# The last batch's main expert, picked by the gate's answer to the mean of its values, with its weights asked for five steps sooner

## The chip, the core and the metric

The kernel runs on one core of a Trainium2 chip. The metric is device time in microseconds, the median of several runs. One execution was also taken by the hardware profiler; its rows are what the text reads. Engines in those rows: PE is TensorE, PEld its weight loads, DVE is VectorE, ACT is ScalarE, POOL is GpSimd, SP is SyncE, which here only issues DMAs. L261 is line 261 of the kernel's file.

## What is computed

Multi-query attention over 8 batches, 16 heads, 384 positions and a head dimension of 64, all heads sharing one k and v; then a mixture of experts with a two-level gate, one expert for each of the 3072 tokens:

```python
scores = scale * np.matmul(q, k.transpose(0, 1, 3, 2))
attn = softmax(scores)                          
x = (attn @ v).transpose(0, 2, 1, 3).reshape(3072, 1024)
g_idx = argmax(x @ w_group)
e_idx = argmax(x @ w_expert[g_idx])
h = np.maximum(x @ w1[g_idx, e_idx], 0.0)
out = g_w * e_w * (h @ w2[g_idx, e_idx])
```

q, k and v are drawn with a standard deviation of 0.1, so scores are close to zero, attention is close to uniform and a token's row is close to the mean of its batch's v, repeated for the 16 heads. Worked out from the inputs, all 384 tokens of each of batches 0 to 6 choose one expert; in batch 7 363 tokens choose expert 0 and 21 choose expert 2. Expert weights are 4 MB each for w1 and w2 in fp32 and are turned to bf16 by the DMA that loads them.

## The kernel before

**Steps.** The attention is cut into tiles of 128 positions (`t`, 24 of them, three to a batch) and each tile into 4 steps, so there are 96 steps `i`, 12 to a batch; `s0` is a batch's first step (84 for batch 7). A step computes the scores of 4 heads (`scores`, L210), takes the maxima on DVE (`nmx`, L221), the exponentials on ACT (L224), the reciprocal of their sums on DVE (`rinv`, L235) and multiplies by it on POOL (`norm`, L239). Two steps later DVE transposes the result in blocks into a ring (`transp`, L245). The third and fourth step of a tile multiply the ring of the tile before by v on TensorE (`pv`, L261); `pv_out` copies the result on ACT and casts it on POOL to the bf16 tokens `xb`.

**Order.** The order on each engine is that of the program text; nothing is reordered. `at(step, place, function, ...)` puts a call at a named place of a step, and `run(i, place)` in the loop executes it. In the order of a step the places are: `s`, `b` (between the two score halves), then for a tile's first two steps `m0`, a group of expert work, `m1`, another, `m3`; then `v`, `m2`, the two transpositions, `w`, `norm`, `e`, `pv_out` in a tile's last step, and `g`. So `w` is ahead of the step's normalisation on DVE and POOL, and `g` behind it.

**Experts.** Each batch has a main expert, which is computed for all 384 tokens with weights zeroed for the tokens that chose another. `main_expert(b)` is a generator that `advance` moves in groups of 8 matmuls or so between the steps of the next batch: first `h` (L483, 64 matmuls), then `y` (L497, 48 matmuls), then scaling by the gate (L515 on ACT or L517 on DVE) and the writes to the output (L541, on SP; for the last tile of batch 7 half of them on ACT). Batch 6's expert begins in step 89, and both its last part and batch 7's whole expert run after the loop, in the drain.

**Picking the main expert.** When a batch's first tile of tokens exists, at step `s0 + 8`, `logits` (L284) computes its gate logits, `gate_first` marks each token's expert, `gate_choose` counts them with a matmul against ones (L345), `gate_score` and `gate_pick` find the expert with the highest count (ties by the lower number), and `load_main` reads that number into a POOL register (`value_load`) and issues the weights' DMAs, two for each of w1 and w2 (`load_w`, L458). For batches 0 to 6 this all is issued at `g` of step `s0 + 9`, for batch 7 w1 at `w` of step 93 and w2 at `w` of step 94. The pools hold two buffers for w1 and two for w2.

**Leftovers.** For batch 7 a second expert is picked (`gate_pick_second`: the highest count once the main expert's is taken out), its weights are loaded (`load_second(0)` for w1, `load_second(1)` for w2), and up to 32 of its tokens are gathered, computed at the end (`few_expert`, L677 for its matmuls, L693 for the scaling) and scattered into the output by an indirect DMA from POOL (L694). What is still not covered, by count, goes to a loop of a length known only on the chip (L909), which reads tokens back from a scratch in HBM that `keep_xb` (L474) fills for each batch. In the profiled execution it runs zero times.

**Buffers that matter here.** `xbank()` hands out four PSUM banks in turn, to the gate, the expert and `pv` (which takes all four); `scores` has two of its own. `transp` of a step reads what `norm` wrote two steps before.

## Time and profile before

| | us |
|---|---|
| median of 3 runs | 507.48 |
| lowest, highest run | 504.97, 507.82 |
| the profiled execution, its own time | 507.47 |
| its span, first to last instruction | 506.0 |
| TensorE busy | 479.9 (95%) |
| VectorE busy | 412.6 (82%) |
| ScalarE busy | 319.6 (63%) |
| GpSimd busy | 288.4 (57%) |
| mean granted TensorE clock, share of full | 0.986 |

In the rows of the timeline and of the groups the columns are: start and duration in us, engine, line, operation, what is written and what it is read from, the shapes, the number of instructions, and in brackets the idle time of the engine before and what ended it. In the chain of waits a row is a stretch of the chain that ended last: start, length, what it was. The answers about one line give "duration ns min/median/max, first and last start us" and, for DMAs, the time from issue to landing.

Places in time that the text speaks of: batch 7's first step, 84, has its scores at 395.52 us, step 85 at 400.53, step 88 at 413.99, step 93 at 438.79, and step 95, the last, at 448.50.

### The profile page before, as it was taken

To read this page: it belongs to the slowest core of one execution; us is meant where nothing else is said; L and a number is where in the kernel's file an instruction comes from. 1 tells how busy PE (TensorE), PEld (TensorE's weight loads), DVE (VectorE), ACT (ScalarE), POOL (GpSimd) and SP (SyncE) were. 2 spreads that over 40 slices of the span, in tenths; PEclk is the share of its full clock that TensorE was granted. 3 is DMA by queue.
4 is the path that set the end of the run, shared out by engine and by line. 5 is a ranking of instruction groups with operands and counts; after the bars stand their busy time and mean duration, and the time that the engine had idled before them with its cause. 6 is when DMAs were issued, how large, how long until landed. Compare 5 with 4: busy or idle time off the path is not lost.

```text
span 506.0 us, 20018 instructions
## 1 busy us (share of the span) xinstructions
PE 479.9 (95%) x8249; PEld 257.5 (51%) x8249; DVE 412.6 (82%) x738; ACT 319.6 (63%) x997; POOL 288.4 (57%) x528
## 2 busy tenths in 40 slices
PE   7687789999999999999999999999999999999992
PEld 3144355555455455555555455554555455555651
DVE  3899979998799888998799888898799888891441
ACT  4776756766765775766765875766766766662420
POOL 1656865585476654685476654684566653674210
PEclk9799999999999999999999999999999999999997
DMA  7522899389955999479965999279964995069995
GB/s 111 121 45 43 150 237 222 74 135 230 252 121 102 208 244 240 80 136 229 242 137 93 203 247 254 54 138 225 227 175 78 197 240 159 3 117 228 242 225 181
DMA packets 63660, 84.04 MB, mean 166 GB/s; under 512 B 20280, under 2 KB 39868, under 8 KB 63312
## 3 DMA queue, kind: packets, MB, share of 16 engines
q0 software_dynamic: 18288, 37.84, 41.2%
q1 hardware_dynamic: 44224, 44.35, 35.1%
q8 instruction: 66, 1.08, 0.9%
q10 hardware_dynamic: 1056, 0.56, 0.5%
q14 instruction: 26, 0.21, 0.1%
HBM read 101.52 MB, written 19.01 MB: 238 GB/s over the span
## 4 chain that ended last, share of the span: by engine, by line
PE 88%; DVE 4%; ACT 2%; DMA 2%; issue 1%; POOL 0%; SPq 0%; POOLq 0%; ACTq 0%; DVEq 0%
PE x L261 26%; PE s L210 26%; PE x L483 15%; PE x L497 13%; PE sb L497 3%; PE x L284 3%; ACT pr L224 2%; DVE nmx L221 2%; PE sb L483 2%; DMA out_dram<-y 2%; DVE ring L245 1%; PE x L104 1%; PE x L149 0%; PE x L187 0%; PE x L598 0%
## 5 line engine op out<-in xcount | busy, mean ns | idle before, releaser
L239 POOL TENSOR_SCALAR pr<-pr,rinv 128x384 f32<-128x384 f32 x384 | 217.3, 585 | 149.1 <-DVE rinv L235 135.9
L224 ACT ACTIVATE pr<-s,nmx 128x384 f32<-128x384 f32 x384 | 218.0, 579 | 132.2 <-DVE nmx L221 122.4
L221 DVE TENSOR_REDUCE nmx<-s 128x2 f32<-128x768 f32 x192 | 174.5, 949 | 47.2 <-PE s L210 46.3
L245 DVE STREAM_TRANSPOSE ring<-pr 128x768 f32<-128x768 f32 x192 | 175.4, 952 | 0.1
L210 PE MATMUL s<-kt,qt 64*64 64x384 f32 x1536 | 151.3, 504 | 12.0 <-ACT pr L224 9.9
L261 PE MATMUL x<-ring,v_sb 32*64 32x256 f32 x4608 | 137.9, 378 | 0.4 <-issue 0.3
L261 PEld LDWEIGHTS x<-ring,v_sb 32*64 32x64 f32 x4608 | 101.2, 131 | 43.7 <-issue 23.7
L210 PEld LDWEIGHTS s<-kt,qt 64*64 64x64 f32 x1536 | 48.8, 133 | 83.0 <-ACT pr L224 44.4
L224 ACT ACTIVATION_READ_ACCUMULATOR pr<-s,nmx 128x1 f32 x384 | 77.8, 203 | 0.0
L483 PE MATMUL x<-xb,w 128*128 128x384 bf16 x448 | 76.6, 326 | 0.0
L483 PEld LDWEIGHTS <-w 128*128 128x128 bf16 x512 | 47.7, 98 | 42.2 <-issue 12.6
L497 PE MATMUL x<-w,h_t 128*128 128x512 bf16 x288 | 65.3, 380 | 0.0
L497 PEld LDWEIGHTS <-h_t 128*128 128x128 bf16 x384 | 35.7, 98 | 51.9 <-issue 11.9
L458 POOL DMA_DIRECT2D w<-in_moe_w_dram x36 | 27.4, 767 | 10.7 <-issue 8.8
L275 ACT COPY xt<-x 128x256 f32<-128x256 f32 x96 | 28.9, 385 | 3.3 <-PE x L261 3.3
L489 ACT ACTIVATE h_t<-x 128x384 bf16<-128x384 f32 x56 | 25.4, 502 | 6.6 <-PE x L483 6.6
L276 POOL CAST xb<-xt 128x1024 bf16<-128x1024 f32 x24 | 24.9, 1036 | 3.4 <-ACT xt L275 3.4
L515 ACT ACTIVATE y<-x,gsel 128x512 f32<-128x512 f32 x36 | 24.8, 693 | 3.1 <-PE x L497 3.1
L199 DVE STREAM_TRANSPOSE qt<-q_sb 128x512 f32<-128x512 f32 x38 | 26.1, 687 | 0.0
L497 PE MATMUL sb<-w,h_t 128*128 128x512 bf16 x96 | 21.5, 379 | 0.0
L235 DVE RECIPROCAL rinv<-ssum 128x4 f32<-128x4 f32 x96 | 13.9, 145 | 3.3 <-ACT pr L224 3.3
L515 ACT ACTIVATE y<-sb,gsel 128x512 f32<-128x512 f32 x9 | 6.2, 689 | 15.7 <-PE sb L497 15.7
(129 smaller groups left out, 153.0 us busy)
## 6 DMA issues: line engine op xcount, KB each, us to landing
w<-in_moe_w_dram POOLq DMA_DIRECT2D x36, 1024.0 KB, 19.4
q_sb<-in_q_dram SPq DMA_DIRECT2D x76, 224.0 KB, 6.0
out_dram<-y SPq DMA_DIRECT2D x94, 128.0 KB, 6.4
xb_scratch<-xb SPq DMA_DIRECT2D x8, 768.0 KB, 4.3
v_sb<-in_v_dram SPq DMA_DIRECT2D x32, 96.0 KB, 3.7
kk<-in_k_dram SPq DMA_DIRECT2D x28, 92.0 KB, 4.1
q_sb<-in_q_dram SPq DMA_DIRECT2D x16, 128.0 KB, 3.4
q_sb<-in_q_dram SPq DMA_DIRECT2D x5, 64.0 KB, 3.0
```

The lines of the kernel that those rows point to most:

```text
L199: nc.vector.transpose(out=qt[:].rearrange("p (x d) -> p x d", d=32), in_=q_sb[:, :, 0:32])
L210: nc.tensor.matmul(out=s[m * D:(m + 1) * D, h, 0:S], lhsT=qt[r, ts(2 * cc + m, D)], rhs=kt[r, :], start=True, stop=True, tile_position=(h ...
L221: nc.vector.tensor_reduce(out=nmx[:], in_=s[:, :, 0:S], axis=AX.X, op=ALU.max, negate=True)
L224: nc.scalar.activation(out=pr[:, h, :], in_=s[:, h, 0:S], func=ACTF.Exp, bias=nmx[:, h:h + 1], scale=1.0, accum_out=ssum[:, k, h:h + 1],)
L239: nc.gpsimd.tensor_scalar(out=pr, in0=pr, scalar1=rinv[:, k, h:h + 1], scalar2=1.0, op0=ALU.mult, op1=ALU.mult)
L245: nc.vector.transpose(out=ring[:, (u // 4) % 3, u % 4].rearrange("p h s -> p (h s)"), in_=st.pop(("pr", u))[:].rearrange("p h s -> p (h s)"),)
L261: nc.tensor.matmul(out=o[i][h * D:(h + 1) * D, 0:2 * P].rearrange("d (g c q) -> d g c q", g=2, c=4), lhsT=v_sb[r, n, :], rhs=ring[r, a:z + ...
L275: nc.scalar.copy(out=xt[:, :, ts(i, 32)], in_=o[:, 0:2 * P].rearrange("p (c q) -> p c q", c=KO))
L458: nc.gpsimd.dma_start(out=w[:, o:o + 4, :], in_=views[n][ds(e, 1), :, o:o + 4, :].rearrange("o p c f -> (o p) c f"))
L483: nc.tensor.matmul(out=hp[:, 0:S], lhsT=w1[:, ko, ts(fc, P)], rhs=xb[:, ko, :], start=(ko == 0), stop=(ko == KO - 1))
L497: nc.tensor.matmul(out=yp, lhsT=h_t[:, fo, ts(j, P)], rhs=w2[:, fo, ts(nh, 512)], start=(fo == 0), stop=(fo == FO - 1),)
L515: nc.scalar.activation(out=y[:, ts(nh, 512)], in_=yp, func=ACTF.Copy, scale=g)
```

## The change

`gate_first` gets a number of partitions, so that it can work on 32 as on 128. For batch 7 a guess is made before any of its tokens exist. `guess_sum` adds up the 12 rows of v that each partition holds (DVE, `w` of step 81). `guess_mean` sums them over the partitions with two matmuls against a column of ones, one for each half of the partitions, so that the sum stands twice, as two heads have it, and copies it to 32 columns (TensorE and ACT, `m3` of step 84). `guess_logits` multiplies it with the gate's weights, 8 matmuls into one 32 x 32 block (`m3` of step 85); `guess_first` transposes the block and marks its expert on 32 partitions (DVE, `w` of step 85). Then the old functions count, score and pick at step 88. The weights are issued at `g` of steps 88 (w1) and 89 (w2) instead of `w` of steps 93 and 94.

The first tile's gate is still evaluated at step 93, now only for the second pick, which moves from the drain into `w` of step 94; `load_second(0)` moves from the drain to `g` of step 95. `keep_xb` of batch 7 moves from the end to just behind the last `pv_out`.

```diff
-    def gate_first(b):
+    def gate_first(b, n=P):
 
-        L = st["lg", b][:, 0, 0:NL].rearrange("p (g e) -> p g e", e=4)
+        L = st["lg", b][0:n, 0, 0:NL].rearrange("p (g e) -> p g e", e=4)
...
-        st["first", b] = first
+        st["first", b] = first, n
...
+        first, n = st.pop(("first", b))
         nc.tensor.matmul(
-            out=c_ps[:, 0:GE], lhsT=ones[:], rhs=st.pop(("first", b))[:].rearrange("p g e -> p (g e)"),
-            start=True, stop=True,
+            out=c_ps[:, 0:GE], lhsT=ones[0:n, :], rhs=first.rearrange("p g e -> p (g e)"), start=True, stop=True
         )
         st["c_ps", b] = c_ps
+
+    def guess_sum(b):
+        vs = pool.tile([P, D], FP32, tag="vs", name="vs", bufs=1)
+        nc.vector.tensor_reduce(out=vs[:], in_=st["v", b][:].rearrange("p n d -> p d n"), axis=AX.X, op=ALU.add)
+        st["vs"] = vs
+
+    def guess_mean():
+
+        vs = st.pop("vs")
+        bank = xbank()
+        for h in range(2):
+            nc.tensor.matmul(
+                out=bank[ts(h, D), 0:1], lhsT=vs[:], rhs=one[:], start=True, stop=True, tile_position=(0, h * D)
+            )
+        mean = pool.tile([P, 32], FP32, tag="mean", name="mean", bufs=1)
+        nc.scalar.copy(out=mean[:], in_=bank[:, 0:1].to_broadcast([P, 32]))
+        st["mean"] = mean
+
+    def guess_logits():
+
+        mean = st.pop("mean")
+        bank = xbank()
+        for ko in range(KO):
+            nc.tensor.matmul(
+                out=bank[0:32, 0:32], lhsT=wge[:, ko, :], rhs=mean[:], start=(ko == 0), stop=(ko == KO - 1),
+                tile_position=(0, 0),
+            )
+        st["guess"] = bank
+
+    def guess_first(b):
+        lg = pool.tile([P, ST, 32], FP32, tag="lg", name="guess_lg")
+        nc.vector.transpose(out=lg[0:32, 0, :], in_=st.pop("guess")[0:32, 0:32])
+        st["lg", b] = lg
+        gate_first(b, 32)
...
         at(s0 + 9, "w", gate_score, b)
-        at(s0 + 9, "w", gate_pick, b)
-        at(s0 + (13 if b == B - 1 else 12), "w", gate_picked, b)
         if b == B - 1:
-            at(s0 + 9, "w", load_main, b, 0)
-            at(s0 + 10, "w", load_main, b, 1)
+            at(s0 - 3, "w", guess_sum, b)
+            at(s0, "m3", guess_mean)
+            at(s0 + 1, "m3", guess_logits)
+            at(s0 + 1, "w", guess_first, b)
+            at(s0 + 4, "m3", gate_choose, b)
+            at(s0 + 4, "w", gate_score, b)
+            at(s0 + 4, "w", gate_pick, b)
+            at(s0 + 5, "w", gate_picked, b)
+            at(s0 + 4, "g", load_main, b, 0)
+            at(s0 + 5, "g", load_main, b, 1)
+            at(s0 + 10, "w", gate_pick_second, b)
+            at(s0 + 11, "g", load_second, 0)
         else:
+            at(s0 + 9, "w", gate_pick, b)
+            at(s0 + 12, "w", gate_picked, b)
...
-        if b == B - 1:
-            at(s0 + 13, "w", gate_pick_second, b)
...
+    one = singles.tile([P, 1], FP32)
+    nc.vector.memset(one[:], 1.0)
...
     transp(2 * i - 2)
     transp(2 * i - 1)
-    run(i + 1, "w")
     advance(1)
-    load_second(0)
     few_ready()
...
     pv_out(NT - 1)
+    keep_xb(b)
     advance(1)
     load_second(1)
...
     advance(1000)
-    keep_xb(b)
     few_expert()
```

More of the change, by code (lines that the diff above doesn't have):

```diff
@@ L300 @@
     NG = ST * (1 + G)
[L302 to L309 removed]
+    def gate_first(b, n=P):
+        L = st["lg", b][0:n, 0, 0:NL].rearrange("p (g e) -> p g e", e=4)
+        mx = pool.tile([P, 1 + G], FP32, tag="g_mx0", name="mx", bufs=1)[0:n]
+        nc.vector.tensor_reduce(out=mx, in_=L, axis=AX.X, op=ALU.max)
+        oh = pool.tile([P, 1 + G, 4], FP32, tag="g_oh0", name="oh", bufs=1)[0:n]
+        nc.vector.tensor_tensor(out=oh, in0=L, in1=mx.unsqueeze(2).to_broadcast([n, 1 + G, 4]), op=ALU.is_ge)
+        first = pool.tile([P, G, Eg], BF16, tag="g_first", name="first", bufs=1)[0:n]
         nc.vector.tensor_tensor(
[L311 removed]
+            out=first, in0=oh[:, 1:1 + G, :], in1=oh[:, 0, :].unsqueeze(2).to_broadcast([n, G, Eg]), op=ALU.mult
         )
[L313 removed]
+        st["first", b] = first, n
     def gate_masks(b):
```

6 lines of the change are left out of this document (removed).

## The prediction

> **What bounds the kernel now.** I read a table of stretches near the end first (busy time of each engine, the granted TensorE clock, the DMA engines' share), then what TensorE waited for, then the chain of waits in order of time.
>
> ```profile
> core 0: us, PE busy (x) PEld busy (x) DVE busy (x) ACT busy (x) POOL busy (x), PEclk, DMA share, GB/s
> ...
> 430.00:443.00 13.00, 13.00 (x242) 7.28 (x235) 11.60 (x23) 8.84 (x30) 8.79 (x17) 1.00 0.01 3
> ...
> 470.00:494.00 24.00, 24.00 (x232) 14.01 (x231) 11.48 (x45) 8.63 (x17) 4.51 (x17) 1.00 1.08 232
> 494.00:506.00 12.00, 2.27 (x66) 1.52 (x64) 1.98 (x4) 0.00 (x0) 1.11 (x1) 0.70 0.51 173
> ```
> ```profile
> PE x L261 <- issue: 0.3, 1, 0.3
> ```
> The last fence is the whole list of TensorE's waits between 380 and 494 us: a single one of 0.3 us, with nothing behind it that the profile shows. TensorE is full from 430 to 443 us, when the DMA engines lie idle (share 0.01), and just as full from 470 to 494 us, when they are saturated (1.08, weights still coming in). So the last weights crowd each other on the DMA engines, but no matmul is seen waiting for them. Only behind 494 us is TensorE off the path. The chain shows what follows there:
>
> ```profile
> 438.17 0.69 PE x L284 x50
> ...
> 440.31 2.71 PE x L483 x16
> 443.02 0.01 PE x L345
> ...
> 477.89 5.20 PE sb L483 x32
> ...
> 488.53 6.91 DMA out_dram<-y
> ...
> 496.28 2.91 DMA out_dram<-y
> ...
> 500.43 1.04 POOL out_dram L694
> ```
> The last write of `y` lands at 496.28 + 2.91 = 499.19 us, and only then does POOL scatter the second expert's few rows (L694), because both write the output tensor.
>
> When do the weights land, and when are they read? Here are the issues of the main expert's w1, its w2, and the second expert's w2, each with its time to landing:
>
> ```profile
> L458 POOL DMA_DIRECT2D w<-in_moe_w_dram x2: 753/786/819, 446.0 to 446.8; - x2
> ...
> DMA to landing us min/median/max: 8.0/10.6/13.1
> ```
> ```profile
> L458 POOL DMA_DIRECT2D w<-in_moe_w_dram x2: 759/774/788, 449.8 to 450.6; - x2
> ...
> DMA to landing us min/median/max: 17.3/20.1/22.9
> ```
> ```profile
> L458 POOL DMA_DIRECT2D w<-in_moe_w_dram x2: 547/570/593, 470.3 to 470.9; - x2
> ...
> DMA to landing us min/median/max: 19.4/21.9/24.4
> ```
> ```profile
> 470.96 1.47 PE L483 MATMUL sb<-xb,w 128*128 128x384 bf16 x8
> ...
> 483.65 3.61 PE L497 MATMUL sb<-w,h_t 128*128 128x512 bf16 x16
> ...
> 496.09 1.06 PE L677 MATMUL x<-w,xg 128*32 128x256 bf16 x32 [0.88 <-DVE xg L691]
> ```
> Main w1 is in at 446.8 + 13.1 = 459.9, read from 470.96: 11 us to spare. Main w2 is in at 473.5, read from 483.65: 10 us. The second w2 is in at 495.3 and read from 496.09: 0.8 us, and the row names DVE, not a DMA, as the last to come. The change asks for main w1 and w2 some 25 and 21 us sooner (below). That buys TensorE nothing directly; it empties the DMA queues under the last 12 us.
>
> **What the change gains.** Main w1 goes out behind the normalisation of step s0+4, main w2 behind that of s0+5, into the idle stretch. The second expert's w1 goes from the drain to the end of the last loop step. Its w2 stays where it is, at 470.3, because batch 6's expert reads that buffer until then. With 3 of the 4 loads gone by then, it should take about the 13.1 us of the first pair's second half, the least crowded load shown: in at 471 + 13 = 484 us rather than 495.3. No weights are then under way when batch 7's outputs leave. How fast such writes land then is shown by four of batch 5, issued after its weights were in:
>
> ```profile
> L541 SPq DMA_DIRECT2D out_dram<-y x4: 315/422/1056, 419.8 to 421.7; - x4
> ...
> DMA to landing us min/median/max: 2.1/2.3/2.7
> ```
> ```profile
> L541 ACTq DMA_DIRECT2D out_dram<-y x2: 350/481/612, 495.1 to 495.5; - x2
> ```
> ```profile
> 494.26 0.75 DVE L517 TENSOR_SCALAR y<-sb,gsel 128x512 f32<-128x512 f32 x1 [2.70 <-PE sb L497]
> ...
> 497.21 0.48 DVE L693 TENSOR_SCALAR rest<-x,c 128x256 f32<-128x256 f32 x1 [1.17 <-PE x L677]
> ```
> The last `y` is ready at 495.0; ACT issues its two writes at 495.1 and 495.5. SP should do the same, but it issued its last one only at 496.28, since its queue was still working off the row before, whose writes took 6.91 us and gate the next ones. Without that crowd SP's last also goes out at 495.5 and lands 2.1 to 2.7 us later: 497.6 to 498.2 instead of 499.19, a gain of 1.0 to 1.6, taken as 1.2. The second expert's result, ready at 497.7, caps this at 1.5. The Trainium skill, "DMA: Bandwidth & Descriptors", section "Anatomy of one DMA — SWDGE (gpsimd) path", fits a DMA as 2.0 us plus bytes at 436 GB/s; by it four writes of 128 KB under way together take an estimated 3.2 us, and the gain would be 0.5. No row of four such writes alone is that long, so the rows decide.
>
> Moving `keep_xb(7)` puts its 768 KB write behind the cast of the last `xb`, ahead of batch 6's last outputs on SP. Those come from an expert group that runs later in program order, so SP holds nobody up. At its old place it competed with the scatter; here are its issue with its landing, and the scatter's landing:
>
> ```profile
> L474 SPq DMA_DIRECT2D xb_scratch<-xb x1: 354/354/354, 497.1 to 497.1; - x1
> ...
> DMA to landing us min/median/max: 5.6/5.6/5.6
> ```
> ```profile
> DMA to landing us min/median/max: 2.5/2.5/2.5
> ```
> `keep_xb(7)` is in at 502.7, the scatter at 500.4 + 2.5 = 502.9, and for that landing all engines wait. Gain between 0 and 0.4 (2.5 against the 2.1 of the shortest write), taken as 0.2. Together **1.4 us** gained, ends 1.0 and 1.9. Taking POOL's wait for the expert's number out of step s0+9 frees POOL, not TensorE: nothing.
>
> **What it costs.** TensorE has no idle time in the loop, so every matmul added shows.
>
> ```profile
> L284 PEld LDWEIGHTS x<-xt,wge x64: 106/109/113, 438.1 to 438.6; 128*32 128x32 f32 x64
> L284 PE MATMUL x<-xt,wge x64: 196/196/217, 438.1 to 438.7; 128*32 128x32 f32 x64
> ```
> - `guess_logits`: 8 fp32 matmuls of 32 columns on one tile position. L284 runs 32 fp32 matmuls in 64 records, 0.69 us in the chain, four tile positions in turn: 16 records per position, 43 ns each. One position with nothing between its loads can be slower. Ends: 16 x 43 = 0.69 and, if each load (109 ns) and matmul (196 ns) came strictly one behind another, 16 x 305 = 4.9. I take 0.9, near the low end, whose row has the same shape and type.
> - `guess_mean`, 2 matmuls or 4 records: 0.2 (4 x 43, upper end 1.2). The extra `gate_choose`: 0.01 by L345. Its copy on ACT falls where ACT waits for the next step's maxima.
>
> ```profile
> 388.15 1.78 DVE L221 TENSOR_REDUCE nmx<-s 128x2 f32<-128x768 f32 x2
> ...
> 390.85 0.58 ACT L224 ACTIVATE pr<-s,nmx 128x384 f32<-128x384 f32 x1
> ...
> 391.29 1.52 PE L210 MATMUL s<-kt,qt 64*64 64x384 f32 x16
> ```
> - `guess_sum` on DVE, 768 strided values: L221 takes 0.89 for as many, so 1.0. It lands in step 81, just ahead of this row, before which DVE has no idle time. 0.9 late, the last exponential ends at 392.3 instead of 391.4; the second half of the next scores, which reuse that buffer, is due at 391.29 + 0.76 = 392.05. Stall 0.2, ends 0 and 1.0.
>
> ```profile
> 404.96 0.14 DVE L235 RECIPROCAL rinv<-ssum 128x4 f32<-128x4 f32 x1
> 405.10 0.71 DVE L199 STREAM_TRANSPOSE qt<-q_sb 128x512 f32<-128x512 f32 x1
> ...
> 405.54 1.52 PE L210 MATMUL s<-kt,qt 64*64 64x384 f32 x16
> ...
> 406.48 1.82 DVE L221 TENSOR_REDUCE nmx<-s 128x2 f32<-128x768 f32 x2 [0.67 <-PE s L210]
> ...
> 409.76 1.52 PE L210 MATMUL s<-kt,qt 64*64 64x384 f32 x16
> ```
> - `guess_first` makes DVE stand in step 85 until `guess_logits` is through. Queued behind it: `rinv` (so POOL's normalisation), the query transposition, the next step's maxima (so ACT, so the scores after). TensorE reaches the guess at 405.5 and leaves it at 406.4; four gate operations of an estimated 0.2 (by `rinv`'s 0.14) take DVE to 407.2, `rinv` and the query to 408.1, so the maxima start there instead of at 406.48. In step 82 the last exponential ended 3.3 us after its maxima began, which makes it 411.4 here; the scores that need its buffer are due at 409.76 + 1.1 + 0.76 = 411.6. Covered by 0.2: cost 0. If it isn't, each microsecond of it goes to the end.
>
> ```profile
> 430.22 2.26 POOL L239 TENSOR_SCALAR pr<-pr,rinv 128x384 f32<-128x384 f32 x4 [1.83 <-DVE es L420]
> ```
> - POOL's pair of issues for main w2 takes 2 x 0.77 = 1.55 us and falls into the 1.83 us that POOL idles there; the pair for w1 comes a step earlier, ahead of the gate's masks. Cost 0; uncovered, 1.5 us on the normalisation, which nothing reads for two steps. The guess's score and pick are 4 more DVE operations of 0.2, in a step whose next maxima wait for TensorE. The second pick, now in step 94, delays only the last normalisation, and 24 of the expert's matmuls stand before TensorE's next use of it: 0.
>
> Sum of costs 0.9 + 0.2 + 0.2 = **1.3 us**, ends 0.7 and 7.1 (4.9 + 1.2 + 1.0). Net 1.3 - 1.4 = -0.1 on the profiled execution's 507.47 us (span 506.0 and 1.5 around it), which is within 0.01 of the median 507.48. **Forecast 507.4 us.** The three runs spread from 504.97 to 507.82, so about 1% is what a measurement can tell from no change.
>
> **Rivals.**
> 1. *The guess runs serially on TensorE* (slower). The eight matmuls accumulate in one place, with no other tile position to fill in. Against it: L483, also 8 to a sum at one position, runs at 2.71 / 16 = 169 ns each with loads hidden. At the upper end, 4.9 + 0.2 + 0.2 and 0.3 more for DVE behind it, less 1.4: 507.5 + 4.2 = 511.7; it costs more than the tail gives from 1.0 us on. Chance 0.16.
> 2. *The weights were a hidden bound* (faster). The busy rows could hide waits; if the second expert's w2, with 0.8 us to spare here, is late in other runs, the tail gains more. Against it: L483 runs at 163 ns in the crowded stretch (5.20 / 32) and at 169 with idle DMA engines. The Trainium skill's sentence, "Trainium Kernel Development and Optimization", "Performance Expectations", that matmul busy time is a bad metric is the general form of this doubt; the start-to-start spacing speaks against it here. It would give the tail's whole 1.9 and 1 to 2 us of lateness less 1.3: about 505.4. Chance 0.12.
> 3. *The guess names another expert.* The mean's gate logits, worked out from the inputs, choose expert 0, which 363 of batch 7's 384 tokens take; the runner-up in its group is 0.00016 behind. A miss sends 363 tokens through the loop for leftovers: one more load of some 25 us and an expert of 64 x 0.163 + 48 x 0.22 = 21 us: about 553. Chance 0.02.
>
> **How the numbers follow.** Forecast 0.68, rivals 0.16, 0.12, 0.02, and 0.02 for anything else. The forecast's own range is 507.4 less 1.2 (the gain's upper and the costs' lower end) and plus about 1, widened by the spread of the runs: 505 to 509. To leave out no more than 2 in 10 I go down to rival 2's 504.6 and into rival 1 up to 510.3. Over 1% faster means under 502.4, which the 12 us tail cannot give: 0.05. Over 1% slower means above 512.5, only the far end of rival 1 and rival 3: 0.09. Within 1%: 0.86.
>
> **What would show it.** The last loads issued near 421, 428 and 457 us; DMA share above 0.9 in the former idle stretch; batch 7's writes landing in 2 to 3 us; the scatter starting about 1.2 us sooner after the last main-expert matmul; that matmul itself about 1.3 us later. Wrong if TensorE's last main-expert matmul moves earlier, if guess_logits takes over 2 us, or if the loop for leftovers runs.

## The result and the profile after

| | before | changed |
|---|---|---|
| median, us (runs) | 506.39 (8) | 510.96 (8) |
| lowest, highest run | 504.97, 507.82 | 508.32, 512.53 |
| the profiled execution, its own time | 507.47 | 511.33 |
| its span | 506.0 | 509.9 |
| TensorE busy | 479.9 | 480.6 |

The ratio is 1.0082 [1.0055, 1.0109]: the change costs about 4 us, where 507.4 was forecast, with a range up to 510.3. The forecast started from the first three runs' 507.48; as a change it was -0.1 us. The same kernel on another chip (e9 below) gave 1.0072 [1.0046, 1.0097]. The 8 runs of before hold the 3 of the table ahead of the prediction.

First the changed kernel's stretches, in the columns of the prediction's first fence; the bounds are not moved along with the steps: at 380 us the changed execution is 0.7 us ahead of before's, at 430 us some 2 us behind, in the tail 4.6.

```profile
core 0: us, PE busy (x) PEld busy (x) DVE busy (x) ACT busy (x) POOL busy (x), PEclk, DMA share, GB/s
380.00:395.00 15.00, 14.20 (x307) 8.16 (x313) 14.72 (x28) 8.56 (x28) 8.95 (x16) 1.00 0.47 90
...
430.00:443.00 13.00, 12.19 (x290) 6.97 (x277) 10.84 (x18) 9.01 (x30) 9.34 (x19) 1.00 1.12 212
...
498.00:510.00 12.00, 2.85 (x68) 1.73 (x66) 1.98 (x4) 0.00 (x0) 1.11 (x1) 0.81 0.27 78
```

The weights went where they were sent: the stretch from 430 to 443 us has a DMA share of 1.12 instead of 0.01, and the last 12 us only 0.27 instead of 0.51. But TensorE, which had no idle time from 430 to 443 us, now stands for 0.81 us there, and for 0.80 between 380 and 395. Its list of waits from 380 to 500 us (total, times, longest), which held one of 0.3 us before:

```profile
PE s L210 <- issue: 0.8, 1, 0.8
PE s L210 <- ACT pr L224: 0.8, 2, 0.6
PE sb L517 <- issue: 0.8, 1, 0.8
PE x L261 <- issue: 0.7, 1, 0.7
```

Three of the five have no releaser at all ("issue"). Here they stand in order of time, from the timeline of TensorE and VectorE, with the guess; the last fence is before's row for step 88:

```profile
386.77 1.50 DVE L353 TENSOR_REDUCE vs<-v_sb 128x64 f32<-128x768 f32 x1
...
391.17 0.88 PE L210 MATMUL s<-kt,qt 64*64 64x384 f32 x8 [0.56 <-ACT pr L224]
...
392.30 0.88 PE L210 MATMUL s<-kt,qt 64*64 64x384 f32 x8 [0.25 <-ACT pr L224]
...
406.11 0.69 PE L373 MATMUL x<-mean,wge 128*32 128x32 f32 x16
...
406.84 0.20 DVE L381 STREAM_TRANSPOSE guess_lg<-x 32x32 f32<-32x32 f32 x1 [1.23 <-PE x L373]
...
415.30 2.26 PE L210 MATMUL s<-kt,qt 64*64 64x384 f32 x16
...
434.21 0.80 PE L210 MATMUL s<-kt,qt 64*64 64x384 f32 x2 [0.81 <-issue]
...
468.66 1.55 PE L261 MATMUL x<-ring,v_sb 32*64 32x256 f32 x48 [0.71 <-issue]
...
475.56 1.46 PE L517 MATMUL sb<-xb,w 128*128 128x384 bf16 x8 [0.76 <-issue]
```
```profile
413.99 1.52 PE L210 MATMUL s<-kt,qt 64*64 64x384 f32 x16
```

`guess_sum` is L353, `guess_logits` L373, the transposition of the guess L381; L517 and L531 are the expert's matmuls (L483 and L497 before). Laid step against step over before's trace, the lateness (how much longer a step takes than the same step before; it can be more than the stall listed: in e2 below 96 matmuls take 0.76 longer with no stall) comes from: both halves of step 83's scores, which wait for ACT behind `guess_sum` (steps 82 and 83 take 0.63 and 0.48 longer); `guess_mean` 0.21; `guess_logits` 0.62; the step behind DVE's wait 0.12; step 88, whose 16 score matmuls took 2.26 us instead of 1.52, 0.85; step 91 with its 0.81 stall, 1.61; the drain with stalls of 0.71 and 0.76, 0.82 more than before, which has one of 0.3. The sum is 5.3; less the 0.7 that this execution was ahead, 4.6.

The tail gives little back. The chain of waits there:

```profile
498.85 0.76 DVE y L551
...
500.35 2.84 DMA out_dram<-y
...
504.35 1.04 POOL out_dram L728
```

The second expert's first matmuls, from the timelines of the changed kernel and of before:

```profile
498.74 1.06 PE L711 MATMUL x<-w,xg 128*32 128x256 bf16 x32
```
```profile
494.15 1.06 PE L677 MATMUL x<-w,xg 128*32 128x256 bf16 x32
```

Counted from there, the last output write leaves 1.61 us later (2.13 before) and takes 2.84 (2.91 before); the span ends 11.15 us later instead of 11.83. That is a gain of 0.68 where 1.4 was expected.

### The profile page after: what moved, and what is told of

Same layout as the page of the kernel before. It is cut to its first block, busy times and chain, and to the rows that moved or that the text cites. A ratio compares the mean times of both kernels' runs of the same rounds, so it can differ in the third digit from the quotient of the medians.

```text
span 509.9 us, 20046 instructions
## 1 busy us (share of the span) xinstructions
PE 480.6 (94%) x8253; PEld 258.4 (51%) x8270; DVE 414.6 (81%) x745; ACT 319.6 (63%) x998; POOL 288.3 (57%) x528
## 4 chain that ended last, share of the span: by engine, by line
PE 85%; DVE 6%; ACT 4%; issue 2%; DMA 2%; SPq 0%; POOL 0%; POOLq 0%; ACTq 0%; DVEq 0%
PE x L261 25%; PE s L210 25%; PE x L517 13%; PE x L531 12%; ACT pr L224 3%; PE sb L531 3%; DVE nmx L221 3%; PE x L284 2%; PE sb L517 2%; DVE ring L245 2%; DMA out_dram<-y 1%; DMA q_sb<-in_q_dram 1%; PE x L104 1%; DVE y L551 0%; PE x L187 0%
## 5 line engine op out<-in xcount | busy, mean ns | idle before, releaser
L221 DVE TENSOR_REDUCE nmx<-s 128x2 f32<-128x768 f32 x192 | 174.6, 948 | 45.6 <-PE s L210 44.5
L210 PE MATMUL s<-kt,qt 64*64 64x384 f32 x1536 | 152.9, 504 | 13.6 <-ACT pr L224 11.9
L517 PE MATMUL x<-xb,w 128*128 128x384 bf16 x448 | 76.6, 327 | 0.0
L517 PEld LDWEIGHTS <-w 128*128 128x128 bf16 x512 | 47.6, 98 | 43.0 <-issue 13.4
L531 PE MATMUL x<-w,h_t 128*128 128x512 bf16 x275 | 64.5, 380 | 0.6
L531 PEld LDWEIGHTS <-h_t 128*128 128x128 bf16 x384 | 35.7, 98 | 52.0 <-issue 11.9
L531 PE MATMUL sb<-w,h_t 128*128 128x512 bf16 x92 | 21.3, 380 | 0.2
```

The source lines that it names most:

```text
L210: nc.tensor.matmul(out=s[m * D:(m + 1) * D, h, 0:S], lhsT=qt[r, ts(2 * cc + m, D)], rhs=kt[r, :], start=True, stop=True, tile_position=(h ...
L221: nc.vector.tensor_reduce(out=nmx[:], in_=s[:, :, 0:S], axis=AX.X, op=ALU.max, negate=True)
L517: nc.tensor.matmul(out=hp[:, 0:S], lhsT=w1[:, ko, ts(fc, P)], rhs=xb[:, ko, :], start=(ko == 0), stop=(ko == KO - 1))
L531: nc.tensor.matmul(out=yp, lhsT=h_t[:, fo, ts(j, P)], rhs=w2[:, fo, ts(nh, 512)], start=(fo == 0), stop=(fo == FO - 1),)
```

## Experiments

Each was timed in five rounds beside the kernel before on the same chip; e1 to e4, e5 to e8, e9 to e12, e13 to e15, e16 and e17, and e18 each shared a chip. Kernels with "constant 0" take expert 0 for batch 7 from a tile `known`, set at the start, instead of picking it; the pick that is then made late only serves the second pick. The microseconds are the ratio's distance from 1, or the difference of two ratios, times the median of before, about 506.

**e9: the change again.**

> The changed kernel as it is, once more, beside the others. If the stalls behind instruction fetches belong to the program (the same 16 KB packets meet the same weight loads in every execution), the ratio is again 1.007 to 1.010, and the profile again shows TensorE waits without a cause of 0.7 to 1.0 us in the step that runs under main w1 and w2, and one or two of 0.3 to 0.8 in the drain. If they belong to one execution only, the profile shows them elsewhere or not at all, and the ratio falls to 1.004 or below, which is what the added work alone costs.

510.18 against 506.15, 1.0072 [1.0046, 1.0097]. The stalls belong to the program, their sizes to the execution: steps 82 to 85 lost the same 0.63, 0.48, 0.21 and 0.62, step 88 lost 0.82 (0.85), step 91 only 0.45 (1.61), the drain 0.57 (0.82), all against before's trace. So a profiled execution alone doesn't give these terms; the ratios below do.

### The parts of the change

**e1: the weights late again.**

```diff
-            at(s0 + 4, "g", load_main, b, 0)
-            at(s0 + 5, "g", load_main, b, 1)
+            at(s0 + 9, "w", load_main, b, 0)
+            at(s0 + 10, "w", load_main, b, 1)
```

> The changed kernel with its guess and all its other moves, but the main expert's weights asked for where they were before (steps 93 and 94). Theory A (two causes: the guess's own work on the engines, some 2.9 us by the profile, and about 2 us of TensorE gaps that come from the weights now crowding the DMA engines in steps 88 to 92): about 2.5 to 3 us over the kernel before, about 1.5 to 2 under the changed kernel; no gap without a cause between 425 and 445 us. Theory B (only the guess's work costs, the gaps are chance): as slow as the changed kernel or slower, 4.5 over before. Theory C (only the crowd on the DMA engines costs): the time of the kernel before.

508.89 against 506.5, 1.0048 [1.003, 1.0066], so 2.4 us are left without the early loads. The DMA engines idle again in the stretch around 430 us, and the timeline of TensorE shows steps 91 and 92 at before's distance, 4.23 us, with no stall:

```profile
429.75 1.52 PE L210 MATMUL s<-kt,qt 64*64 64x384 f32 x16
431.20 2.85 PE L261 MATMUL x<-ring,v_sb 32*64 32x256 f32 x96
433.98 1.52 PE L210 MATMUL s<-kt,qt 64*64 64x384 f32 x16
```

**e2: the early main weights alone (constant 0).**

```diff
+    known = singles.tile([P, 1], I32)
+    nc.gpsimd.memset(known[:], 0)
...
-            at(s0 + 9, "w", load_main, b, 0)
-            at(s0 + 10, "w", load_main, b, 1)
+            at(s0 + 4, "g", load_main, b, 0)
+            at(s0 + 5, "g", load_main, b, 1)
```

> The kernel before, with batch 7's main-expert weights asked for at steps 88 and 89 as in the change, the expert's number being a constant 0 in place of the gate's pick for that load alone (the gate still picks for everything else); no guess, nothing else moved. Theory A: 0 to 1.5 us over the kernel before: gaps of TensorE of up to 2 us less a shorter tail of about 0.8; a gap of 0.5 to 1 us between 425 and 445 us that ends 1.3 to 1.5 us behind an instruction fetch. Theory B: 0.8 us faster than before, no such gap. Theory C: 4 us slower.

506.25 against 506.5, 0.9997 [0.9981, 1.0013]. Nothing in sum, but the trace shows a loss and a gain. Between steps 91 and 92 it loses 0.77 us, since `pv` of step 91 takes 3.61 us instead of 2.85:

```profile
428.37 1.52 PE L210 MATMUL s<-kt,qt 64*64 64x384 f32 x16
429.82 3.61 PE L261 MATMUL x<-ring,v_sb 32*64 32x256 f32 x96
433.36 1.52 PE L210 MATMUL s<-kt,qt 64*64 64x384 f32 x16
```

And from step 95 to the second expert's first matmul it takes 44.68 us, before 45.65. There before has the one wait of 0.3 us that the prediction's list showed without a cause, and e2 has none:

```profile
462.62 2.37 PE L261 MATMUL x<-ring,v_sb 32*64 32x256 f32 x69
465.33 1.11 PE L261 MATMUL x<-ring,v_sb 32*64 32x256 f32 x27 [0.34 <-issue]
```

So before's own drain is 0.97 us late, and the early main weights take that away. The tail is not shorter (11.99 us): `keep_xb`, still at the end, is now issued earlier and runs beside the last output writes.

**e5: the scratch write early, alone**, in the kernel before.

```diff
     pv_out(NT - 1)
+    keep_xb(b)
...
     advance(1000)
-    keep_xb(b)
     few_expert()
```

> The kernel before with one move alone: batch 7's tokens go to the scratch right behind the last pv_out, as in the change, instead of at the very end; the weights are asked for where they were. Theory D (the tail's gain of 0.6 to 0.7 us comes from this write no longer colliding with the last output writes): 0.5 to 0.8 us faster than before, last main-expert matmul to the end 0.5 us or more shorter. The prediction's view (the weights' crowd is what costs the tail 1.2, this write 0.2): at most 0.2 us faster.

508.38 against 505.97, 1.0053 [1.0033, 1.0074]: slower by 2.7 us, which neither side expected. In the crowd of that kernel 768 KB more make the second expert's w2 late, and its matmuls wait, as the timeline shows:

```profile
495.69 0.62 PE L677 MATMUL x<-w,xg 128*32 128x256 bf16 x16 [0.88 <-DVE xg L691]
497.68 0.64 PE L677 MATMUL x<-w,xg 128*32 128x256 bf16 x16 [1.36 <-DMA w<-in_moe_w_dram]
```

The 0.8 us to spare that the prediction found for that load were all there was.

**e6: all moves, no guess (constant 0).** The change with the guess taken out: early main weights, early second pick and w1, early scratch write. Against the change:

```diff
-            at(s0 - 3, "w", guess_sum, b)
-            at(s0, "m3", guess_mean)
-            at(s0 + 1, "m3", guess_logits)
-            at(s0 + 1, "w", guess_first, b)
-            at(s0 + 4, "m3", gate_choose, b)
...
+            idx = known if b == B - 1 else st.pop(("idx", b))
+            st["e", b] = nc.gpsimd.value_load(idx[0:1, 0:1], min_val=0, max_val=GE - 1)
```

> All moves of the change, without the guess: the expert's number for batch 7's main weights is a constant 0, the gate picks for the rest. Weights at steps 88 and 89, second pick at step 94, its w1 at step 95, the scratch write behind the last pv_out. Theory A with D: 0.6 to 1.2 us faster than before (what the moves can bring at best), so the guess's work and the TensorE gaps that come with it are the whole loss. If the moves themselves cost: the time of the kernel before or slower.

507.33 against 505.97, 1.0016 [1.0001, 1.0032]. Even without the guess the moves cost 0.8 us, though the tail is 0.7 us shorter (11.17).

**e10: e2 with the scratch write behind the gather (constant 0).**

```diff
     few_gather()
     advance(2)
+    keep_xb(b)
...
     advance(1000)
-    keep_xb(b)
     few_expert()
```

> Before's kernel with expert 0 for batch 7 written in as a constant and its weights issued at the end of steps 88 and 89 (no guess), and with the write of the tokens to the scratch moved behind the gathering of the second expert's few tokens, so that it is neither in the tail nor in front of the gather. Theory: in e2 the emptier queue was given back because that write collided with the last outputs; with the write out of the tail, few_expert's first matmul to the end takes 11.1 to 11.4 us instead of 12.0, and the time is 0.6 to 0.9 below e2: ratio 0.998, 505.6. Rival (the tail's gain does not come from the write's place): the tail stays at 12, ratio 1.000.

505.6 against 506.15, 0.9982 [0.997, 0.9994], as expected, with a tail of 11.13 us; the trace loses 0.79 in step 91 and gains 0.97 in the drain, as e2's. Early weights and a scratch write outside the tail together give the tail's 0.7; neither does it alone. It is the only version whose interval lies below 1, and its expert is written in; no version that picks the expert was faster than before.

### The guess

**e12: `guess_sum` alone**, in the kernel before, its result unused.

```diff
         if b == B - 1:
+            at(s0 - 3, "w", guess_sum, b)
```

> Before's kernel with guess_sum alone, at its place in step 81, its result unused; nothing else is changed. Theory: it holds up the maxima and with them the exponentials of step 81 long enough for two of the next scores to wait, +1.1 us (0.9 to 1.3), ratio 1.002. The prediction's step said 0.2, ratio 1.000. If the time rises by more than 1.5, the later part of the loop pays for the shift too.

507.25 against 506.15, 1.002 [1.0006, 1.0035]: 1.0 us by the ratio, 1.1 by the medians. The timeline shows the stall of the change again, line by line:

```profile
384.96 1.51 DVE L353 TENSOR_REDUCE vs<-v_sb 128x64 f32<-128x768 f32 x1
...
389.38 0.88 PE L210 MATMUL s<-kt,qt 64*64 64x384 f32 x8 [0.57 <-ACT pr L224]
...
390.50 0.88 PE L210 MATMUL s<-kt,qt 64*64 64x384 f32 x8 [0.25 <-ACT pr L224]
```

**e3: `guess_sum` in four pieces** of 16 columns, at steps 79, 80, 82 and 83.

```diff
-            at(s0 - 3, "w", guess_sum, b)
+            for c, x in enumerate((5, 4, 2, 1)):
+                at(s0 - x, "w", guess_sum, b, c)
```

> The changed kernel with the sum over v done in four pieces of 16 columns at steps 79, 80, 82 and 83 instead of one instruction of 1.5 us in step 81. Theory A and B: TensorE's stall of about 1.1 us in steps 82 and 83 goes, so 0.8 to 1.1 us faster than the changed kernel. Theory C: the changed kernel's time.

508.17 against 506.5, 1.0036 [1.002, 1.0052]. The stall in steps 82 and 83 is gone. The difference to the change is 1.8 to 2.3 us, more than the 1.1 of e12, with intervals that leave room for 1.1. In the traces of e3 and e7 step 91 loses nothing, which can be the rest.

**e4: `guess_first` one step later**, at `e` of step 86, so that DVE doesn't wait for the guess.

```diff
-            at(s0 + 1, "w", guess_first, b)
+            at(s0 + 2, "e", guess_first, b)
```

> The changed kernel with the guess's transposition and marking on VectorE moved from step 85, where they wait for TensorE, to the end of step 86, where their input is long ready. Theory A and B: the wait of 1.2 us on VectorE goes, and with it the 0.9 us that the scores of steps 87 and 88 lose, so 0.7 to 0.9 us faster than the changed kernel, scores of step 88 in 1.5 us instead of 2.2. Theory C: the changed kernel's time.

515.26 against 506.5, 1.0161 [1.0135, 1.0187], a miss in direction. `pv` of step 86 takes all four banks of `xbank()`, and one still holds the guess:

```profile
408.79 0.67 PE L261 MATMUL x<-ring,v_sb 32*64 32x256 f32 x12
412.06 2.20 PE L261 MATMUL x<-ring,v_sb 32*64 32x256 f32 x72 [2.59 <-DVE guess_lg L381]
```

**e7: e3 with `guess_logits` at `m0` instead of `m3` of step 85**, so that DVE finds it done.

```diff
-            at(s0 + 1, "m3", guess_logits)
+            at(s0 + 1, "m0", guess_logits)
```

> The changed kernel with the sum in four pieces at steps 79, 80, 82 and 83, and the guess's 8 matmuls ahead of step 85's two expert groups instead of behind them, so that VectorE finds their result ready. Theory A: VectorE's wait of 1.2 us goes, TensorE still pays 0.6 for the matmuls: 0 to 0.4 us under the variant with the sum in pieces, 1.2 to 1.8 us over the kernel before. If VectorE's wait was what TensorE lost in steps 87 and 88 (0.9): 0.9 under that variant.

508.39 against 505.97, 1.004 [1.0022, 1.0057], no better than e3: DVE's wait for the guess costs nothing that can be measured.

**e11: the smallest guess.** e3's pieces, the gate's weights added up over the heads once at step 8, so that one matmul takes the place of eight, and e10's scratch write.

```diff
-        for ko in range(KO):
-            nc.tensor.matmul(
-                out=bank[0:32, 0:32], lhsT=wge[:, ko, :], rhs=mean[:], start=(ko == 0), stop=(ko == KO - 1),
-                tile_position=(0, 0),
-            )
+        nc.tensor.matmul(
+            out=bank[0:32, 0:32], lhsT=st.pop("wsum"), rhs=mean[:], start=True, stop=True, tile_position=(0, 0)
+        )
```

> The change with all that the runs so far showed as a cost made small: guess_sum in four pieces of 16 columns in four steps, the gate's weights summed over the heads once at step 8, so that the guess is one matmul instead of eight, and the scratch write behind the gathering. The outputs are the same. Theory: guess_sum costs 0, the guess 0.1 to 0.2 instead of 0.7, DVE does not wait; what is left is guess_mean's 0.2 and the slow fetches under the moved weights (0.5 to 1.0), against a tail gain of 0.7: ratio 1.000 to 1.002, 1.5 to 2 us under e3. Rival (it is the moved loads and the moved second pick, not the guess): ratio 1.004 as e3 and e7.

507.61 against 506.15, 1.0032 [1.0014, 1.0051]. The guess's matmuls now cost TensorE 0.4 us in the trace (DVE still waits 0.79 for their result, though the expectation said that it wouldn't), but the kernel was still 1.6 us slower than before: step 91 alone is 1.14 late, and the drain is 1.15 behind e10's and 0.18 behind before's. So something other than the guess is left, and e6 says the same.

### The fetches

What else differs where TensorE stands without a releaser? The page's list of queues has two that carry instructions, q8 and the smaller q14 (packets of 8 KB). Here is q8 in the changed kernel (packets, MB, share):

```profile
q8 instruction: 66, 1.08, 0.8%
```

The page counts its packets, 16 KB each, among those of the same 16 DMA engines as the data. In all runs each stall of TensorE over 0.15 us without a releaser, in the loop's last steps or the drain, ends 1.2 to 1.6 us after a packet of q8 has arrived, with weights under way; where the engines are idle no stall follows: in e1 three packets are all that moves between 426 and 442 us.

```profile
DMA packets 3, 0.05 MB, mean 3 GB/s; under 512 B 0, under 2 KB 0, under 8 KB 0
## 3 DMA queue, kind: packets, MB, share of 16 engines
q8 instruction: 3, 0.05, 1.3%
```

That is the theory tested next: weights moved under a fetch make the fetch late.

**e8: e2 with the four main loads issued twice**, the second time at steps 91 and 92, into the same buffers.

```diff
             at(s0 + 5, "g", load_main, b, 1)
+            at(s0 + 7, "g", load_again, b, 0)
+            at(s0 + 8, "g", load_again, b, 1)
```

> The kernel before with batch 7's weights asked for at steps 88 and 89 by a constant number, as in the earlier run, and the same 4 loads issued once more into the same tiles at steps 91 and 92: twice the traffic, nothing else. Theory A (instruction fetches of TensorE queue behind weights): one or two more gaps of 0.3 to 1.6 us between steps 88 and 95 or in the drain, each ending 1.2 to 1.6 us behind a fetch; 1 to 3 us slower than with the loads issued once. If a crowd on the DMA engines is harmless to TensorE: the same time as with the loads issued once.

506.89 against 505.97, 1.0014 [0.9995, 1.0032]: 0.9 us above e2, in the direction of the theory, but the intervals overlap. It decides nothing by itself. In the trace its drain's fetch starts 14.59 us after step 95, against 11.61 in e2, and the drain is 0.97 late again, as before's; step 91 is 1.26 late instead of 0.77.

**e13: e10 with the second pick in step 94 and its w1 at the end of step 95 (constant 0).**

```diff
+            at(s0 + 10, "w", gate_pick_second, b)
+            at(s0 + 11, "g", load_second, 0)
...
-    run(i + 1, "w")
     advance(1)
-    load_second(0)
```

> e10 (constant expert 0, main weights at steps 88 and 89, scratch write behind the gather) with the second pick in step 94 and the second w1 issued at the end of step 95, as the change has them. Theory: the second w1 asked for at step 95 flows while TensorE fetches the drain's instructions, which come late by 0.7 to 1.8 us in every run that has it (the change, e3, e6, e11) and by nothing in e2 and e10, which haven't; so 1.0 to 1.8 us above e10, ratio 1.001 to 1.002, and TensorE waits without a cause between 450 and 480 us. Rival (the scratch write's place made the difference between e6 and e10): as e10, ratio 0.998.

507.32 against 506.18, 1.0019 [0.9999, 1.0039], 1.9 us above e10. The two traces agree to 0.01 us from step 95 on, up to one stall. First TensorE's timeline in e10, then in e13:

```profile
449.45 1.52 PE L210 MATMUL s<-kt,qt 64*64 64x384 f32 x16
...
463.57 2.85 PE L261 MATMUL x<-ring,v_sb 32*64 32x256 f32 x96
```
```profile
447.84 1.52 PE L210 MATMUL s<-kt,qt 64*64 64x384 f32 x16
...
461.96 2.37 PE L261 MATMUL x<-ring,v_sb 32*64 32x256 f32 x69
465.03 1.11 PE L261 MATMUL x<-ring,v_sb 32*64 32x256 f32 x27 [0.69 <-issue]
```

The group of 96 matmuls begins 14.12 us after step 95 in both. In e10 it takes 2.85 us; in e13 TensorE stops after 69 of them. All behind it is 1.33 us late, up to the last matmul. Now the issues of the second w1 ("first and last start"), again e10 and then e13:

```profile
L458 POOL DMA_DIRECT2D w<-in_moe_w_dram x2: 751/782/814, 459.8 to 460.6; - x2
```
```profile
L458 POOL DMA_DIRECT2D w<-in_moe_w_dram x2: 751/782/814, 456.0 to 456.9; - x2
```

After step 95 began that is 10.4 us in e10 and 8.2 in e13. And the DMA share, e10 and then e13, in the columns of the stretches:

```profile
458.00:460.00 2.00, 2.00 (x45) 1.21 (x51) 0.54 (x4) 0.72 (x2) 0.19 (x1) 1.00 0.57 129
460.00:462.00 2.00, 2.00 (x74) 1.34 (x59) 0.00 (x0) 0.00 (x0) 1.92 (x5) 1.00 0.82 161
```
```profile
458.00:460.00 2.00, 2.00 (x86) 1.53 (x67) 0.00 (x0) 0.15 (x1) 1.60 (x14) 1.00 0.96 133
460.00:462.00 2.00, 1.95 (x21) 0.74 (x15) 0.00 (x0) 0.00 (x0) 0.66 (x4) 1.00 1.05 197
462.00:464.00 2.00, 2.00 (x70) 1.59 (x70) 0.00 (x0) 0.69 (x1) 0.00 (x0) 1.00 1.11 267
```

By the packets' own records the drain's first fetch started 11.66 us after step 95 in e10, while the engines were still filling up, and took 1.0. In e13 it started only at 14.97, took 0.93, and TensorE went on 1.29 us after its arrival. The load that came 2.2 us sooner pushed the fetch back by 3.3 us, past the point at which TensorE ran out of instructions.

**e15: the change with just the second pick and w1 back in the drain. e14: e11 with the same.** Both edits are e13's, the other way round.

```diff
-            at(s0 + 10, "w", gate_pick_second, b)
-            at(s0 + 11, "g", load_second, 0)
+            at(s0 + 13, "w", gate_pick_second, b)
...
+    run(i + 1, "w")
     advance(1)
+    load_second(0)
```

> The changed kernel with only the second pick and the second expert's w1 back in the drain. Theory: 1.0 to 1.5 us under the change (1.0072 and 1.0082 so far): ratio 1.005 to 1.006, and no TensorE wait without a cause between 450 and 480 us, except under the write of the scratch. Rival (that move is free): ratio 1.0075, the waits in the drain stay.

508.05 against 506.18, 1.004 [1.0021, 1.0059].

> e11 (guess_sum in four pieces, guess of one matmul, scratch write behind the gather) with the second pick and the second w1 back in the drain as in before; outputs as the change's. Theory: the drain's late fetches go, so 1.0 to 1.5 us under e11: ratio 0.999 to 1.001; guess_mean and what is left of the guess then eat e10's gain. Rival (e11's remainder is the guess itself): ratio 1.003 as e11.

506.45 against 506.18, 0.9998 [0.9983, 1.0014]: the changed kernel's whole computation in before's time. In both the drain's fetch starts 10.7 to 11.0 us after step 95 and its stall is gone. Six kernels now stand in a table of two by three:

| ratio to before | second pick and w1 in the drain | in steps 94 and 95 |
|---|---|---|
| no guess (constant 0) | e10 0.9982 | e13 1.0019 |
| smallest guess | e14 0.9998 | e11 1.0032 |
| the change's guess | e15 1.0040 | the change 1.0072, 1.0082 |

Along each row the move costs 0.0037, 0.0034 and 0.0032 to 0.0042, 1.6 to 2.1 us; one such difference is uncertain by 1.2 to 1.7 us (the two intervals taken together), but three agree. In the traces the drain is 1.33 us longer in e13 than in e10, 1.13 longer in e11 than in e14, and 1.54 and 1.79 longer in the change's two than in e15. Down the columns the change's guess costs 0.0053 to 0.0063, 2.7 to 3.2 us, the smallest one 0.7 to 0.8. The kernels of the last row write the scratch right behind the last `pv_out`, the others behind the gather; e6 and e13 differ in that alone and in 0.0003.

**e16: e13 with the second pick alone moved; e17: its w1 alone moved** (the second expert's number written in as 2). Against e13, first e16, then e17:

```diff
-            at(s0 + 11, "g", load_second, 0)
...
     advance(1)
+    load_second(0)
```

```diff
-            at(s0 + 10, "w", gate_pick_second, b)
+            at(s0 + 13, "w", gate_pick_second, b)
...
-            st["e2"] = nc.gpsimd.value_load(st.pop("idx2")[0:1, 0:1], min_val=0, max_val=GE - 1)
+            st["e2"] = nc.gpsimd.value_load(known2[0:1, 0:1], min_val=0, max_val=GE - 1)
...
+    run(i + 1, "w")
     advance(1)
```

> e13 with the second expert's w1 asked for in the drain again, at before's place; only the second pick is in step 94. Theory (the load crowds the fetch): no stall in the drain, ratio 0.998 as e10. Rival (the pick's operations on VectorE hold something up): the stall stays, ratio 1.002 as e13.

507.13 against 505.96, 1.0016 [0.9999, 1.0032], which is the rival's number. (What the expectations of e17 and e18 call step 93 is the last step, 95.)

> e13 with the second pick back in the drain; the second expert's number (2) is written in as a constant, so that its w1 can still be asked for at the end of step 95. Theory: the stall of 0.7 us without a cause and the drain's 1.0 to 1.4 us stay, behind an instruction packet that arrives 15 to 16 us after step 93 began instead of 12 to 13, ratio 1.002 as e13. Rival: ratio 0.998 as e10.

507.14 against 505.96, 1.0023 [1.0009, 1.0037], the theory's number; the fetch starts 14.44 us after step 95, though the stall is smaller in this execution (0.2 us; the drain is 0.84 late). Either move alone brings the cost, so e16 seems to speak for the rival. But in e16 POOL no longer waited for the pick, and the load that was meant to stay went out early all the same, 8.2 us after step 95 at 448.90:

```profile
L458 POOL DMA_DIRECT2D w<-in_moe_w_dram x2: 753/784/814, 457.1 to 457.9; - x2
```

Its timeline has e13's stall at the same matmul:

```profile
463.02 2.37 PE L261 MATMUL x<-ring,v_sb 32*64 32x256 f32 x69
466.02 1.11 PE L261 MATMUL x<-ring,v_sb 32*64 32x256 f32 x27 [0.63 <-issue]
```

**e18: e16 with the load held back**, by four copies of the number, one behind another, where the pick used to stand.

```diff
+    def copy_second():
+        for n in range(4):
+            idx = singles.tile([P, 1], I32, name=f"idx{n}")
+            nc.vector.tensor_copy(out=idx[:], in_=st["idx2"][:, 0:1])
+            st["idx2"] = idx
...
+    copy_second()
     advance(1)
     load_second(0)
```

> e16 with four copies of the second expert's number on VectorE, one behind another, in the drain where the second pick stood, so that POOL issues its w1 10.0 to 10.5 us after step 93 began instead of 8.2. Theory (the load's time against the fetch decides): the instruction packet comes 11 to 12 us after step 93 instead of 14.7, no stall in the drain, ratio 0.998 to 0.999. Rival (the pick's work in step 94 costs it): the stall stays, ratio 1.0016 as e16.

506.0 against 506.69, 0.999 [0.9977, 1.0003]. The pick is as early as in e16, the load goes out 10.3 us after step 95 (449.57) and the fetch starts 11.66 after it. The stall is gone:

```profile
L458 POOL DMA_DIRECT2D w<-in_moe_w_dram x2: 751/782/814, 459.9 to 460.7; - x2
```
```profile
463.69 2.85 PE L261 MATMUL x<-ring,v_sb 32*64 32x256 f32 x96
```

So it is the time of the load against the fetch that decides, not the pick's work: a load issued 2 us *later* makes the kernel 0.0026 (1.3 us) faster than e16. The two intervals overlap a little, but in the traces the drain is 1.26 us shorter; step 91 also differs, by 0.45.

## Why the prediction was wrong

**The sum by its own terms.** The four steps that the runs measured: early main weights -0.0003 (e2); the scratch write out of the tail -0.0015 (e10 less e2); second pick and w1 +0.0037 (e13 less e10); the guess +0.0053 to +0.0063 (the change less e13). They are links of one chain from before to the change, so they add up to its ratio by construction. Two others check them: the moves alone (e6) are +0.0016 and the guess in the other column of the table (e15 less e10) +0.0058, together 0.0074 against 0.0072 and 0.0082. The step of the prediction that failed most is the one that took the moved loads to cost TensorE nothing; the others are mostly sizes of terms.

- **`guess_sum`: "Stall 0.2", was 1.1.** The path was right (DVE's maxima, ACT's exponentials, the buffer of the scores after); the operation was taken as 1.0 us from L221, which reads as many values, and took 1.50. The cover was also counted for one half of the next scores; both halves wait. e12 shows the cost alone, e3 shows that it goes when the sum is cut up. The upper end of that term, 1.0, was near the answer.
- **`guess_mean` 0.2 and `guess_logits` 0.9** were about right: 0.21 and 0.62 in the trace, with 16 records in 0.69 us at one tile position, 43 ns each. Rival 1's serial 4.9 us did not happen; its time of 511.7 is near the measured one by another cause.
- **`guess_first`, covered by 0.2: cost 0.** 0.12 in the trace, nothing in the time (e7 against e3).
- **"The second expert's w1 goes from the drain to the end of the last loop step"** was priced only as a gain, fewer loads under the tail. It cost 1.6 to 2.1 us, the largest step that failed. The sign was in the prediction's own list: the wait of 0.3 us "with nothing behind it that the profile shows" is this stall, already there in before, where the drain is 0.97 us behind e10's. The early main weights take it away (e2), the moved w1 brings it back (e13, 1.33). And the early main weights, taken to touch no matmul, cost 0.77 to 0.80 in step 91 (e2, e10, e13). The queues that the prediction asked about were SP's and POOL's; the one that was hit was the instruction queue, which its quoted stretches of DMA share don't show apart.
- **The gain of 1.4 was 0.7.** The last write went out 0.5 us sooner, not 0.8, and took 2.84 us, not 2.1 to 2.7; four left within 0.7 us. The prediction set against its rows the Trainium skill, "DMA: Bandwidth & Descriptors", section "Anatomy of one DMA — SWDGE (gpsimd) path", by whose fit four such writes take an estimated 3.2 us and the gain is 0.5; the writes took 2.4 to 3.0 here, between the rows of batch 5 (2.1 to 2.7) and that estimate, whose fit is for DMAs that GpSimd issues, while these left on SP and ACT. Counted from the second expert's first matmul the last one landed 0.58 us sooner than before, where the rows gave 1.2 and the estimate 0.5; that the estimate came nearer is in part luck, since the write left 0.3 later than it took. And the gain was put down to the weights' crowd; e2 shows that early weights alone give none of it, e10 that it takes the scratch write's move as well, which was priced at 0.2, and e5 that this move alone costs 2.7.
- **Rivals 2 and 3.** No matmul started sooner for its weights, so rival 2 fell as it stood, though before's weights did cost its drain 0.97 us, by way of a fetch; the loop for leftovers didn't run, so the guess named the right expert. Of the prediction's own signs, the loads, the DMA share above 0.9 and the writes' 2 to 3 us came; the last main-expert matmul, "about 1.3 us later", came 4.6 later.

What is shown and what is argued: that the moved second w1 makes the drain's fetch late and that this costs 1.3 to 2.1 us is shown by e13, e14, e15 and e18. That the early main weights alone make step 91 late is shown by e2, e10 and e13 (0.77 to 0.80), against nothing in before, e1, e5 and e12. That a fetch is the reason there too is argued: in the eight kernels with early weights and no guess, the step loses from 0.77 us (e2, whose fetch starts 0.23 after the step began) up to 1.43 (e16, 0.91 after it), and e3 and e7 (with the guess), whose fetch starts 1.7 to 1.8 before it, lose nothing.

Step 88 is late only in kernels with the guess, by 0.1 to 1.3 us, and the early main weights are not the cause: the change issues them from 424.4 us on, behind that step, and e1, without them, still loses 0.30. A fetch starts 0.84 us ahead of that step in the change, under batch 6's last weights, which land at 419.2; why it costs something there with the guess alone was not tested. Beyond its engine work (1.1, 0.2, 0.6 and 0.1) the guess costs some 0.7 to 1.2 of its 2.7 to 3.2 us; step 88 and what step 91 loses more than e13's 0.80 (1.61 in the change, though only 0.45 in e9) may make that up.

## What to carry over

Idle DMA engines under a busy TensorE are not free room: its instructions come through them, so before weights are moved there, look where the instruction packets lie and keep a big load from starting just ahead of one. Where a bound of the engines has gone and none shows in its place, list the waits that have no releaser and lay them beside the packets of the instruction queue. And move a value that a load waits for only after asking what held that load back: a wait can be what keeps a transfer out of the way.

## What was not expected of the hardware

- A 16 KB instruction packet took 0.9 to 1.7 us in the last 100 us of these runs, mostly about 1, even beside full queues, but it starts late: 3.3 us later in e13 than in e10, for a load that began 2.2 us sooner. TensorE goes on 1.2 to 1.6 us after it has arrived.
- In before, e6, e13, e16 and e17 TensorE stops after the same 69th of 96 matmuls, so the stop belongs to a place in the instruction stream, not to a time. With the change's guess, 21 matmul records more ahead of it, it stops after the 48th (the change, e9, e1, e4); with e11's, 7 more, after the 61st.
- Adding 12 strided values for each of 64 columns took VectorE 1.50 us, against 0.89 for the maxima over as many values of L221. A quarter of it took 0.45 to 0.47 us in e3, so four quarters cost more of VectorE's time, 1.8 us, and the stall that the whole sum caused was gone.
